# A half score tile moved ahead of a whole one, and its ordering moved from GpSimd to TensorE

## The chip, the cores and the metric

The kernel runs on one core of a Trainium2 chip. A core has five engines that run side by side and signal each other through semaphores: TensorE (PE in the profile, with its weight loads listed apart as PEld), VectorE (DVE), ScalarE (ACT), GpSimd (POOL) and SyncE (SP, which here issues DMAs). The metric is device time in microseconds (us), the median of several runs. The profile is one execution recorded by the hardware profiler.

## The reference

One transformer block on 2048 tokens of width 512, in float32: a layer norm, an attention block A of 32 heads of width 16, a gated path B, and their product added to the input.

```python
def _A_ref(x, wqkv, wo):
    qkv = (x @ wqkv).reshape(B, S, 3, H, Dh).transpose(2, 0, 3, 1, 4)
    q, k, v = qkv[0], qkv[1], qkv[2]
    scores = jnp.einsum("bhqd,bhkd->bhqk", q, k) * (Dh ** -0.5)
    p = _softmax(scores, axis=-1)
    o = jnp.einsum("bhqk,bhkd->bhqd", p, v)
    return o.transpose(0, 2, 1, 3).reshape(B, S, D) @ wo

def _B_ref(x, w1, b1, w2, b2):
    h = _gelu(jnp.einsum("bsd,df->bsf", x, w1) + b1)
    return jnp.einsum("bsf,fd->bsd", h, w2) + b2

xn = _layernorm(A_x)
s = _A_ref(xn, A_wqkv, A_wo)
g = _silu(_B_ref(xn, B_w1, B_b1, B_w2, B_b2))
return A_x + s * g
```

## The kernel before

The whole program is written out instruction by instruction in Python, under a manual schedule: each engine executes its instructions in the order of the text. Three parts follow each other. Up to about 478 us the norm, the projections and path B are made. From there to about 1506 us runs the attention loop in the form that the change touches. A last part finishes the attention and multiplies by `wo`.

Attention is done by units: 32 units, each of four heads (a group) and 512 queries. A softmax needs the largest score of each row before the exponentials are taken, so the scores are made twice. The first time ("S" work) they are made with the queries on the partitions, into a tile of 128 x 512 called `ps` in PSUM, and VectorE takes row maxima from it (`s_max`, line 189; it reduces two halves of 256 columns at a time). The second time ("T" work) they are made transposed, with keys on the partitions and the maximum already subtracted through two extra rows of the operands; ScalarE takes the exponential out of PSUM (`t_one`, matmul at line 740, exponential at line 742). Then the exponentials are multiplied by the values ("V" work, `pv_step`, line 805). The S work is done about nine units ahead of the T work.

Heads have width 16, so with the split of float32 into a high and a low part a score contracts over 48 rows (S) or 50 rows (T). One such matmul fills less than half of the array's 128 rows. The kernel therefore places head `a=0` at rows 0 to 63 and head `a=1` at rows 64 to 127, and orders the work so that matmuls on the two row halves stand next to each other.

The loop has a step for each 128 keys of a unit, 16 steps to a unit. A step is a string of letters, read from left to right:

- `T`: one transposed score tile and its exponential. The four of a step use the halves a = 1, 1, 0, 0.
- `S`: one whole score tile, 512 columns, and its reduce. The first `S` of a step takes the head a=0, the second the head a=1 of the same job.
- `X` and `Y`: a third score tile that two heads share. `X` writes the head a=0 into columns 0 to 255, `Y` the head a=1 into columns 256 to 511 of the same PSUM bank; then one reduce reads both. Two steps finish such a job.
- `V`: four matmuls of 32 columns each, that use the array's four column groups.

Since X and Y write one bank from two row halves, Y must not run beside X. Before the change this is ensured by a marker on GpSimd: an empty instruction (line 221) that waits until X is done, and Y waits for the marker. `run_off` then emits small GpSimd work that was put off (copies of the row maxima, lines 251 and 252).

PSUM banks: S, X and Y use three banks in a ring (`s_ring`: `ps_a`, `ps_b`, `ps_x`); X takes one out of the ring, and Y puts it back at the end. The T tiles use four banks in turn, and V has one. A score tile that is made into a bank waits for the reduce that read it last; a T tile waits for the exponential.

At the end of each unit ScalarE copies the result of V out of its bank (line 812). Some steps also hold a transpose of the row maxima (line 268) and a last reduction over them (line 248). GpSimd issues key loads (lines 109 and 112) and divisions (line 843) at fixed places of the order.

```python
ORDER = {0: "TTTTV", 3: "TXSTTSTYV"}
for op in ORDER[want] if n > 1 else ("TTTTV", "TTSTSVT")[n]:
    if op in "SXY":
        s_op(op)
```

Of the kernel before, what the change touches and what calls it, by code (L numbers as in the profile page):

```python
# [36 lines left out]
FILL0 = 30  # L37
HB = 4
W2B = 2
ORDER = {0: "TTTTV", 3: "TXSTTSTYV"}  # L40
HC = CH // 2
PAIRED = 28
KB = 3
# [5 lines left out]
def fused(ctx: ExitStack, tc: tile.TileContext, x, wqk, wv, wo, w1, b1, w2, b2, out):  # L49
    nc = tc.nc  # L50
# [35 lines left out]
    SYNC = mybir.DependencyInfo(mybir.DependencyClass.Sync, mybir.DependencyReason.DATA)  # L86
# [5 lines left out]
    def s_tile(held=False):  # L92
        pool = s_ring.pop(0)
        if not held:
            s_ring.append(pool)
        return pool.tile([P, CH], F32, name="ps"), pool
# [58 lines left out]
    done = {u: 0 for u in range(NU)}  # L155
# [16 lines left out]
    def at_of(job):  # L172
        u, st, p = job
        return divmod(st, NCH) if u % (NCH * KB) else divmod(st, NCH)[::-1]

    def s_mm(ps, job, a, c0, k0, w):
        u, st, p = job
        qi, ki = at_of(job)
        if u not in MX:
            MX[u] = qring.tile([P, GH, NCH, NCH, 2], F32, name="mx")  # L180
        r = slice(64 * a, 64 * a + 3 * DH)
        k0 += ki * CH
        return nc.tensor.matmul(ps[:, c0:c0 + w], QS[u][r, p, qi * P:(qi + 1) * P],  # L183
                                kts[u // NCH % KB][p][r, k0:k0 + w], start=True, stop=True).ins

    def s_max(ps, job, heads, parts):
        u, p = job[0], job[2]
        qi, ki = at_of(job)
        nc.vector.tensor_reduce(MX[u][:, 2 * p:2 * p + 2, qi, ki][:, heads, parts], ps.rearrange("p (n c) -> p n c", c=HC), axis=AX.X, op=OP.max)  # L189
        done[u] += 1  # L190
        if ended:
            s_end0(ended.pop())
        if done[u] == 64:
            ended.append(u)
        if done[NU - 1] == 64:
            s_end0(ended.pop())

    def s_whole(job, a):
        ps = s_tile()[0]
        s_mm(ps, job, a, 0, 0, CH)  # L200
        s_max(ps, job, a, slice(0, 2))
# [5 lines left out]
    jobs, whole, cut, put_off = [], [], [], []  # L207

    def s_op(op):
        if op == "S":  # L210
            if whole:
                s_whole(whole.pop(), 1)
            else:
                whole.append(jobs.pop(0))
                s_whole(whole[0], 0)
        elif op == "X":
            if not cut:
                cut[:] = [jobs.pop(0), 0]
            ps, pool = s_tile(True)
            x = s_mm(ps, cut[0], 0, 0, cut[1] * HC, HC)  # L220
            token = nc.gpsimd.nop().ins
            tc.add_manual_dep(token, x.name, SYNC, reason="row tile done")
            cut[2:] = [ps, pool, token]
            run_off()
        else:
            job, n, ps, pool, token = cut
            y = s_mm(ps, job, 1, HC, n * HC, HC)
            tc.add_manual_dep(y, token.name, SYNC, reason="other row tile")
            s_max(ps, job, slice(0, 2), n)
            s_ring.append(pool)  # L230
            cut[1] += 1
            if n:
                cut.clear()

    def run_off():
        while put_off:
            put_off.pop(0)()
# [76 lines left out]
    for j in range(len(pairs)):  # L314
        for h in range(2):
# [9 lines left out]
            n = 2 if nd < len(parts) and parts[nd][2] and ready - nd > room else 1  # L325
            n = max(n, need - 2 * (left - 1))
# [233 lines left out]
    s_when, put, row = [], [0], [0, 0]  # L560
# [387 lines left out]
    for t in range(NW):  # L948
        n = DONE + 2 * t
# [6 lines left out]
    for i, t in enumerate(late):  # L956
        n = L - 2 * len(late) - 1 + 2 * i
# [9 lines left out]
    for n in range(L + 1):  # L967
        ua, ka = divmod(n, 16)
        want = due(n) - due(n - 1)
        i = 0  # L970
# [3 lines that stand above are left out]
            elif op == "V":  # L974
                if n:
                    pv_step(*divmod(n - 1, 16))
                for _ in range(4):
                    tick()
                flush()
            else:  # L980
                if EARLY <= 4 * n + i < 4 * L:
                    t_one(ua, ka, i % 2, 1 - i // 2)
                for f, args in todo.get((n, i), []):
                    f(*args)
                i += 1
# [54 lines left out]
```

## Time and profile before

| | us |
|---|---|
| median of 3 runs | 1596.2 |
| lowest and highest run | 1596.11, 1596.48 |
| span of the profiled execution | 1594.7 |
| TensorE busy | 1587.6 |
| VectorE busy | 1382.8 |
| ScalarE busy | 1260.1 |
| GpSimd busy | 373.0 |

The profiled execution's own time is its span; the runs' times also hold what lies around it. The page gives busy time, then tenths of busy time in 40 slices, the chain of work that ended last, and groups of instructions. In the rows of a group or of the timeline, `ps<-kt,slot` is the output and the inputs by the program's names. A row of the timeline starts with start time and length in us, then engine, line, operation, names, shapes and count; in square brackets stands how long the engine was idle before it and what ended that. Matmul ends are modelled by the profiler, not observed. In the view of one line, the columns are the count, then the shortest, median and longest duration in ns, then the start of the first and of the last. In the view by stretches, the columns are the stretch, its length, the busy time and count of TensorE's matmuls, its weight loads, VectorE, ScalarE and GpSimd, the granted TensorE clock, the DMA share and GB/s.

### The profile page before, as it was taken

Reading aid. Unit: us, or ns where it says so; the run is one execution under the profiler, and the core shown is the slowest. Engines: PE = TensorE matmul, PEld = TensorE weight load, DVE = VectorE, ACT = ScalarE, POOL = GpSimd, SP = SyncE. Lnnn points to the kernel's source line nnn. Section 1 sums busy time; section 2 is a strip of 40 time slices with the busy share of each in tenths; the row PEclk is TensorE's granted clock in tenths of the full one; section 3 lists DMA queues with packets and bytes.
Section 4 is the critical chain, followed back from the end, with each engine's and each line's share of the span. In section 5 each row is a group of like instructions: output and inputs, shape, how many; then the busy total and the mean of one; then the engine's idle time right before and its main releaser. Section 6 shows DMA issues by size and latency. Waiting matters only on the chain.

```text
span 1594.7 us, 32234 instructions
## 1 busy us (share of the span) xinstructions
PE 1587.6 (100%) x12144; PEld 913.2 (57%) x12144; DVE 1382.8 (87%) x2261; ACT 1260.1 (79%) x2520; POOL 373.0 (23%) x394
## 2 busy tenths in 40 slices
PE   9999999999999999999999999999999999999998
PEld 8899999999884444444444444444444444444445
DVE  7598898989888999999999989999999999999735
ACT  4324333434349999999999999999999999999984
POOL 4145575756650001000100200100010000000142
PEclk9999999999999999999999999999999999999999
DMA  6626343454431113111410411311131111110252
GB/s 205 150 59 164 106 135 107 158 140 123 126 93 54 32 35 66 29 39 44 82 30 21 71 40 30 61 39 29 31 70 30 31 29 36 36 29 22 59 192 100
DMA packets 74651, 116.89 MB, mean 73 GB/s; under 512 B 23012, under 2 KB 24292, under 8 KB 73320
## 3 DMA queue, kind: packets, MB, share of 16 engines
q1 hardware_dynamic: 70748, 101.89, 22.8%
q0 software_dynamic: 3264, 12.35, 3.9%
q8 instruction: 96, 1.57, 0.4%
q14 instruction: 59, 0.48, 0.1%
q10 hardware_dynamic: 484, 0.60, 0.1%
HBM read 84.35 MB, written 25.97 MB: 69 GB/s over the span
## 4 chain that ended last, share of the span: by engine, by line
PE 98%; DVE 1%; DMA 1%; POOL 0%; issue 0%; ACT 0%; SPq 0%; DVEq 0%; POOLq 0%
PE pv L805 32%; PE ps L183 18%; PE pst L740 16%; PE ps L591 12%; PE pst L591 7%; PE ps L740 5%; PE ps L80 3%; PE pv L591 2%; PE ps L459 1%; PE pst L80 1%; DMA raw<-in_wqk 0%; DVE st L418 0%; PE pst L441 0%; DMA xt<-in_x 0%; PE pst L459 0%
## 5 line engine op out<-in xcount | busy, mean ns | idle before, releaser
L189 DVE TENSOR_REDUCE mx<-ps 128x2 f32<-128x512 f32 x2048 | 1299.5, 685 | 149.4 <-PE ps L183 68.8
L742 ACT ACTIVATE slot<-pst 128x512 f32<-128x512 f32 x1533 | 831.0, 612 | 21.6 <-PE pst L740 12.7
L805 PE MATMUL pv<-slot,vsb 128*32 128x512 f32 x4096 | 545.3, 605 | 0.0
L183 PE MATMUL ps<-kt,slot 48*128 48x512 f32 (+1 forms) x1364 | 393.5, 376 | 0.0
L740 PE MATMUL pst<-qt,kt 50*128 50x512 f32 x1149 | 372.7, 432 | 0.6 <-DVE gt L673 0.4
L740 PEld LDWEIGHTS pst<-qt,kt 50*128 50x128 f32 x1149 | 178.6, 184 | 279.9 <-ACT slot L742 264.3
L742 ACT ACTIVATE slot<-ps 128x512 f32<-128x512 f32 x515 | 315.5, 613 | 3.7 <-PE ps L740 0.5
L183 PEld LDWEIGHTS ps<-kt,slot 48*128 48x128 f32 x1364 | 210.6, 184 | 34.8 <-DVE mx L189 21.6
L591 PE MATMUL ps<-slot,w1h 64*128 64x512 f32 x1088 | 218.0, 393 | 0.2 <-ACT junk L605 0.2
L183 PE MATMUL ps<-kt,qz 48*128 48x512 f32 x512 | 212.4, 415 | 0.0
L183 PE MATMUL ps<-slot,slot 48*128 48x512 f32 (+1 forms) x598 | 172.8, 376 | 0.0
L740 PE MATMUL ps<-qt,kt 50*128 50x512 f32 x387 | 160.3, 416 | 0.0
L591 PEld LDWEIGHTS ps<-slot,w1h 64*128 64x128 f32 x1088 | 151.4, 185 | 8.3 <-ACT junk L605 2.7
L805 PEld LDWEIGHTS pv<-slot,vsb 128*32 128x32 f32 x4096 | 80.6, 108 | 120.2 <-issue 112.2
L591 PE MATMUL ps<-slot,w1l 64*128 64x512 f32 x544 | 141.7, 393 | 0.0
L378 POOL TENSOR_TENSOR hl<-hg,hh 128x512 fp32r<-128x512 f32 x76 | 96.7, 1295 | 129.6 <-ACT hh L377 82.5
L605 ACT ACTIVATE junk<-ident_r 1x1 f32<-1x1 f32 x92 | 18.0, 196 | 120.8 <-PE pst L591 113.6
L740 PE MATMUL pst<-qt,slot 50*128 50x512 f32 x384 | 112.5, 415 | 0.0
L251 POOL CAST nmh<-nm 128x16 fp32r<-128x16 f32 x32 | 6.3, 197 | 413.7 <-PE pst L740 184.7
L183 PEld LDWEIGHTS ps<-kt,qz 48*128 48x128 f32 x512 | 93.7, 183 | 16.3
L183 PEld LDWEIGHTS ps<-slot,slot 48*128 48x128 f32 x598 | 92.5, 184 | 15.7 <-DVE mx L189 10.9
L740 PEld LDWEIGHTS ps<-qt,kt 50*128 50x128 f32 x387 | 71.1, 184 | 44.0 <-ACT slot L742 42.8
(159 smaller groups left out, 1699.7 us busy)
## 6 DMA issues: line engine op xcount, KB each, us to landing
raw<-in_w SPq DMA_DIRECT2D x88, 256.0 KB
qk_h<-hh SPq DMA_DIRECT2D x32, 256.0 KB
qk_l<-hl SPq DMA_DIRECT2D x32, 256.0 KB
qt<-qk_h SPq DMA_DIRECT2D x128, 64.0 KB
slot<-qk_h SPq DMA_DIRECT2D x92, 64.0 KB
g_d<-gt POOLq DMA_DIRECT2D x16, 256.0 KB, 3.5
qt<-qk_l SPq DMA_DIRECT2D x64, 64.0 KB
dn<-den_d SPq DMA_DIRECT2D x32, 128.0 KB
```

Source lines behind the costliest of these rows:

```text
L80: nc.tensor.matmul(ps, lhs[a], rhs[b], start=first and n == 0, stop=last and n == 2)
L183: return nc.tensor.matmul(ps[:, c0:c0 + w], QS[u][r, p, qi * P:(qi + 1) * P], kts[u // NCH % KB][p][r, k0:k0 + w], start=True, stop=True).ins
L189: nc.vector.tensor_reduce(MX[u][:, 2 * p:2 * p + 2, qi, ki][:, heads, parts], ps.rearrange("p (n c) -> p n c", c=HC), axis=AX.X, op=OP.max)
L251: nc.gpsimd.tensor_copy(hl[:, 0], nm)
L378: nc.gpsimd.tensor_sub(hl, raw, hh.bitcast(F32))
L459: nc.tensor.matmul(pq["q", g, c], W1[g][i][:, k * P:(k + 1) * P], (xh, xl)[j][c][:, k], start=n == 0 and k == 0, stop=n == 2 and k == KT - 1)
L591: i = nc.tensor.matmul(ps, lhs[r], rhs[r], start=first, stop=last).ins
L605: i = nc.scalar.activation(junk[:, :1], ident_r[:1, :1].bitcast(F32), AF.Copy).ins
L740: nc.tensor.matmul(ps, kts[g % KB][p][r, k * P:(k + 1) * P], QT[u][r, p, :], start=True, stop=True)
L742: nc.scalar.activation(PT[u, k][:, 2 * p + a, :], ps, AF.Exp, scale=SCALE)
L805: nc.tensor.matmul(PV[u][32 * j:32 * j + 32, :], vsb[:, k, h:h + 32], PT[u, k][:, j, :], start=(k == 0), stop=(k == NT - 1))
```

## The change

The step's order becomes `TXSTTYSTV`: Y stands directly behind the third T tile and ahead of the second S. The GpSimd marker is removed. In its place an empty TensorE instruction, called `hold`, is put directly ahead of Y; it waits until X is done, on the semaphore that TensorE's own matmuls raise. The maxima of the shared tile are now emitted ahead of those of the second S, and X's bank goes back into the ring ahead of the second S.

```diff
-ORDER = {0: "TTTTV", 3: "TXSTTSTYV"}
+ORDER = {0: "TTTTV", 3: "TXSTTYSTV"}
...
             x = s_mm(ps, cut[0], 0, 0, cut[1] * HC, HC)
-            token = nc.gpsimd.nop().ins
-            tc.add_manual_dep(token, x.name, SYNC, reason="row tile done")
-            cut[2:] = [ps, pool, token]
+            cut[2:] = [ps, pool, x]
             run_off()
         else:
-            job, n, ps, pool, token = cut
-            y = s_mm(ps, job, 1, HC, n * HC, HC)
-            tc.add_manual_dep(y, token.name, SYNC, reason="other row tile")
+            job, n, ps, pool, x = cut
+            hold = nc.tensor.nop().ins
+            tc.add_manual_dep(hold, x.name, SYNC, reason="row tile done")
+            s_mm(ps, job, 1, HC, n * HC, HC)
             s_max(ps, job, slice(0, 2), n)
             s_ring.append(pool)
             cut[1] += 1
```

## The prediction

> **What bounds the kernel now.** First the page: its head, engine shares, granted clock and the chain that ended last.
>
> ```profile
> span 1594.7 us, 32234 instructions
> ...
> PE 1587.6 (100%) x12144; PEld 913.2 (57%) x12144; DVE 1382.8 (87%) x2261; ACT 1260.1 (79%) x2520; POOL 373.0 (23%) x394
> ...
> PEclk9999999999999999999999999999999999999999
> ...
> PE 98%; DVE 1%; DMA 1%; POOL 0%; issue 0%; ACT 0%; SPq 0%; DVEq 0%; POOLq 0%
> ```
>
> TensorE is the chain, at full clock. A busy PE is not a PE at its peak, so the question is where it stands still inside a step. Next, the line of the POOL marker, which runs once in each step that the change touches, and the stretch of these steps.
>
> ```profile
> L221 POOLq EVENT_SEMAPHORE  x490: 17/17/17, 479.6 to 1505.8; - x164
> ...
> 478.00:1506.30 1028.30, 1028.19 (x7860) 439.98 (x7862) 936.60 (x1538) 1012.25 (x1992) 76.74 (x128) 1.00 0.18 41
> ```
>
> 490 markers from 479.6 to 1505.8 make 489 steps of 1026.2 / 489 = 2.099 us: 64% of the span. ACT (the fourth busy column) and DVE (the third) are nearly full in it too, so they have to be watched. Now the weight loads of one such step, in order of time.
>
> ```profile
> 902.76 0.18 PEld L740 LDWEIGHTS pst<-qt,kt 50*128 50x128 f32 x1 [0.84 <-ACT slot L742]
> 902.76 0.18 PEld L183 LDWEIGHTS ps<-kt,slot 48*128 48x128 f32 x1
> 902.87 0.19 PEld L740 LDWEIGHTS pst<-qt,kt 50*128 50x128 f32 x1
> 902.87 0.19 PEld L183 LDWEIGHTS ps<-kt,slot 48*128 48x128 f32 x1
> 902.99 0.18 PEld L740 LDWEIGHTS pst<-qt,kt 50*128 50x128 f32 x1
> 903.30 0.18 PEld L183 LDWEIGHTS ps<-kt,slot 48*128 48x128 f32 x1
> 903.35 0.18 PEld L740 LDWEIGHTS ps<-qt,kt 50*128 50x128 f32 x1
> 903.41 0.19 PEld L183 LDWEIGHTS ps<-kt,slot 48*128 48x128 f32 x1
> 903.85 0.16 PEld L805 LDWEIGHTS pv<-slot,vsb 128*32 128x32 f32 x8 [0.25 <-issue]
> 904.85 0.18 PEld L740 LDWEIGHTS pst<-qt,kt 50*128 50x128 f32 x1 [0.84 <-ACT slot L742]
> ```
>
> I call the pieces T0, X, S0, T1, T2, S1, T3, Y, V, in program order (S0 and S1 are the two heads' whole tiles). Lower row half of the array: X, S0, T2, T3; upper: T0, T1, S1, Y; the halves work side by side (T0 and X load at the same 902.76). Loads run T0 and X 902.76, T1 and S0 902.87, T2 902.99, then a hole, S1 903.30, T3 903.35, Y 903.41, and V from 903.85 to 904.85: a constant 1.00. Who ends the hole:
>
> ```profile
> 902.57 0.68 DVE L189 TENSOR_REDUCE mx<-ps 128x2 f32<-128x512 f32 x1
> 902.68 0.62 ACT L742 ACTIVATE slot<-ps 128x512 f32<-128x512 f32 x1
> 902.76 0.50 PE L740 MATMUL pst<-qt,kt 50*128 50x512 f32 x1
> 902.76 0.18 PEld L183 LDWEIGHTS ps<-kt,slot 48*128 48x128 f32 x1
> 902.77 0.38 PE L183 MATMUL ps<-kt,slot 48*128 48x256 f32 x1
> ...
> 903.42 1.89 DVE L189 TENSOR_REDUCE mx<-ps 128x2 f32<-128x512 f32 x3 [0.17 <-PE ps L183]
> ```
>
> The third reduce of the step before ends at 902.57 + 0.68 = 903.25 and frees S1's bank: S1's load starts 0.05 later. The same 0.05 stands between the end of T3's older exponential (903.30) and T3's load. The three reduces take 1.89 from S0's arrival, so a short step is followed by a late S1. This shows in neighbouring steps, by V's first load:
>
> ```profile
> 901.76 0.16 PEld L805 LDWEIGHTS pv<-slot,vsb 128*32 128x32 f32 x8 [0.25 <-issue]
> ...
> 905.90 0.16 PEld L805 LDWEIGHTS pv<-slot,vsb 128*32 128x32 f32 x8 [0.23 <-issue]
> ```
>
> 905.90 - 901.76 = 4.14 for two steps, 2.07 each. A step in which S1 doesn't wait:
>
> ```profile
> 817.01 0.18 PEld L740 LDWEIGHTS ps<-qt,slot 50*128 50x128 f32 x1 [0.84 <-ACT slot L742]
> ...
> 817.35 0.18 PEld L183 LDWEIGHTS ps<-kt,slot 48*128 48x128 f32 x1
> ...
> 819.03 0.18 PEld L740 LDWEIGHTS ps<-qt,slot 50*128 50x128 f32 x1 [0.84 <-ACT slot L742]
> ```
>
> 819.03 - 817.01 = 2.02 is TensorE's floor. The last kind is the long step after a unit's end, when ACT has the copy of line 812 to do as well and T3 waits for ACT:
>
> ```profile
> 545.32 0.16 PEld L805 LDWEIGHTS pv<-slot,vsb 128*32 128x32 f32 x8 [0.25 <-ACT os L812]
> ...
> 547.28 0.18 PEld L740 LDWEIGHTS ps<-qt,kt 50*128 50x128 f32 x1 [0.30 <-ACT slot L742]
> ...
> 547.71 0.16 PEld L805 LDWEIGHTS pv<-slot,vsb 128*32 128x32 f32 x8 [0.24 <-issue]
> ...
> L812 ACT ACTIVATE os<-pv 128x512 f32<-128x512 f32 x30 | 18.8, 628 | 0.0
> ```
>
> Its length is 2.39, and 30 of them are 71.7 us. The other 459 steps hold 1026.2 - 71.7 = 954.5, a mean of 2.079. Last, T3's load is followed by V 0.43 later: the price of a whole tile whose weights come last.
>
> **The change part by part.** *Y ahead of S1.* In the upper half the order becomes T0, T1, Y, S1. Y's bank is X's own, so Y waits for no reduce. S1's load moves later by what Y takes, so DVE's release of S1's bank (0.54 after T0's load above) is covered. This part alone would bring steps towards the floor. DVE and ACT do the same work; banks still come free in the order of the reduces (S0, halves, S1 instead of S0, S1, halves), so each of the next tiles waits for the reduce of the same place in the order.
>
> *The marker goes.* 490 POOL instructions of 17 ns vanish. Queued behind them on POOL are the maxima's copies, the divisions and key loads, which may go earlier; none is on the chain (POOL 0% above). I take nothing for it.
>
> *The hold.* TensorE now waits until X has signalled, and Y, S1, T3, V and all after them are queued behind it. So the price is X's signal. When does that come? Two rows, the first asked for the stretch 903.32 to 903.34 alone:
>
> ```profile
> L221 POOLq EVENT_SEMAPHORE  x1: 17/17/17, 903.3 to 903.3; - x1
> ...
> 903.30 0.60 ACT L742 ACTIVATE slot<-pst 128x512 f32<-128x512 f32 x1
> ...
> 903.10 0.51 PE L740 MATMUL pst<-qt,kt 50*128 50x512 f32 x2
> ```
>
> X's own modelled end is 902.77 + 0.38 = 903.15, but the marker, which waits for nothing but X, runs at 903.33, just behind ACT's exponential on T0 (903.30; T0's modelled end is 903.26). So X, half as long, signals behind T0, which was issued ahead of it. The Trainium skill, "TensorE: Matmul & The Clock Gate", Part 3, The mechanism, says that matmuls start and end in strict program order. By that rule X cannot signal ahead of T0 and the sum is the slow one below; by X's modelled end, Y's load could start at 903.20 and the sum would be the floor's, 1572 us.
>
> Now the new step, counted from T0's load. Y's load follows the signal as S1 and T3 follow theirs: about 903.35, 0.59. S1's load follows Y's by 0.11, as S0's (902.87) follows X's (902.76): 0.70. There the price of a late whole tile applies, 0.43 to V: 1.13. With V's 1.00 the step is **2.13** whatever DVE does. T3 starts beside S1 in the other half and ends with it; ACT's release of T3's bank (0.59 above) is covered.
>
> Sum. 459 steps x 2.13 = 977.7. To it come the passes of line 268, which push T0, and with it X's signal, later:
>
> ```profile
> 528.57 0.16 PEld L805 LDWEIGHTS pv<-slot,vsb 128*32 128x32 f32 x8 [0.25 <-issue]
> ...
> 529.76 0.18 PEld L740 LDWEIGHTS pst<-qt,kt 50*128 50x128 f32 x1
> ...
> L268 PE MATMUL pst<-ident_r,nmh 128*64 128x128 f32 (+1 forms) x9 | 2.4, 268 | 0.0
> ...
> L268 PE MATMUL ps<-ident_r,nmh 128*64 128x128 f32 (+1 forms) x4 | 1.1, 267 | 0.0
> ```
>
> T0's load stands 1.19 behind V's instead of 1.00, 13 times: 2.6. The long steps hang on ACT, which gains up to 2.13 - 2.02 = 0.11 in the short step ahead, so I take 2.39 - 0.11 = 2.28: 68.4. Total 977.7 + 2.6 + 68.4 = 1048.7 against 1026.2: +22.5 us. The profiled span is 1594.7; the runs' median, 1596.2, lies 1.5 above it, what lies around the span. 1596.2 + 22.5 = **1619 us**.
>
> *The hold's own cost.* No row shows such a wait of TensorE on itself. Lower bound: it rides on Y's weight load as the marker's wait does now, cost nothing; that is the sum above, and I take it, since Y's load then has no other wait to carry. Upper bound: it is an instruction of its own, as at line 441 (asked for 18.36 to 18.38; then the load behind it):
>
> ```profile
> L441 PEldq EVENT_SEMAPHORE  x1: 51/51/51, 18.4 to 18.4; - x1
> ...
> 18.45 0.14 PEld L441 LDWEIGHTS ps<-ident,xn 128*128 128x128 f32 x1 [0.72 <-PE ps L459]
> ```
>
> The load comes 0.08 behind the wait's start. With a start like the marker's, Y loads at 903.41, 0.65, and the step is 2.19.
>
> **The rivals.** *A wait as an own instruction (A2).* 459 x 2.19 + 2.6 + 30 x 2.22 = 1074.4: +48, **1644 us**. For it: line 441's wait does stand alone. Against it: by the kernel's text, Y's load has no other wait left to carry, and the marker's wait, which it carries now, is gone.
>
> *Faster: the hold is free (B).* If X's signal reaches TensorE so that Y loads by 0.48 (1.00 + 0.48 + 0.11 + 0.43 = 2.02), the order alone counts: 459 x 2.02 + 2.6 + 71.7 = 1001.5, -24.7, **1572 us**. Break-even is a load at 0.54 (903.30). For it: X's modelled end, and that a wait on one's own queue could be met early or be dropped as already in order, so that the change does not do what it says. Against it: the marker's time, later than that point.
>
> *The hold empties TensorE (C).* If it waits for all that was issued, T2 (modelled end 903.61 above) lets Y load at 903.66, 0.90; every step is 2.44 and the sum is 489 x 2.44 + 2.6 = 1195.8: **1766 us**. The skill's "PSUM — Partial Sum Buffer", Engine vs sequencer instructions, says that a nop is the sequencer's and waits for earlier instructions to be dispatched only. By that rule this doesn't happen; no run here shows it.
>
> **How the numbers follow.** Forecast 0.62 (1612 to 1628 for itself: 0.02 either way in Y's load is 9 us), A2 0.18, B 0.11, between B and the forecast, within 0.2% of before (3 us, about what a measurement here can tell), 0.03, C and all that is slower than A2 0.06. The range from 1612 to 1650 takes in the forecast and A2, 0.80. Faster 0.11, same 0.03, slower 0.86 (0.62 + 0.18 + 0.06).
>
> **What would show it.** In the profile after: no line 221 on POOL; S1's load no longer behind a reduce; a hole between T2's and Y's loads ending about 0.59 behind T0's load (0.65: A2; 0.48 or less: B; 0.90: C); plain steps all alike near 2.13 instead of 2.02 and 2.12 in turn; long steps shorter than 2.39. Wrong it would be above all if X's signal came earlier than the POOL marker suggests.

## The result, and the profile after

The changed kernel takes 1619.16 us (median of 4 runs, 1618.95 to 1619.55) against 1596.15 us: a ratio of 1.0145, 95% interval 1.0133 to 1.0158. It is 23.0 us slower; the profiled span, 1617.7 us, is also 23.0 us longer than before.

The page of the kernel after, the lines that answer to those shown of before:

```profile
span 1617.7 us, 31752 instructions
...
PE 1611.4 (100%) x12144; PEld 908.4 (56%) x12144; DVE 1381.0 (85%) x2261; ACT 1268.5 (78%) x2520; POOL 373.1 (23%) x394
...
PEclk9999999999999999999999999999999999999999
...
PE 99%; DVE 1%; DMA 0%; issue 0%; ACT 0%; DVEq 0%
...
L183 PEld LDWEIGHTS ps<-kt,slot 48*128 48x128 f32 x1364 | 201.2, 185 | 55.6 <-PE pst L739 35.9
```

The work is the same (12144 matmuls, 2261 VectorE and 2520 ScalarE instructions) and so is the clock. TensorE is still the chain. What has changed is the last line, by its idle time and what ended it. The same group on the page of the kernel before:

```profile
L183 PEld LDWEIGHTS ps<-kt,slot 48*128 48x128 f32 x1364 | 210.6, 184 | 34.8 <-DVE mx L189 21.6
```

This is the larger of two groups of line 183. It idled 34.8 us with DVE the main releaser; now it idles 55.6 us, and the main releaser is TensorE itself. The attribution to line 739 (the T tiles) is inferred by the profile; the wait put into the program is on X. Lines behind the edit are one lower than before: 739 is T, 741 its exponential, 804 V, 811 the copy at a unit's end.

TensorE's weight loads in two steps of the kernel after, in order of time (start, length, operation, what ended the idle time ahead):

```profile
901.75 0.18 PEld L739 LDWEIGHTS pst<-qt,kt 50*128 50x128 f32 x1 [0.84 <-ACT slot L741]
901.76 0.18 PEld L183 LDWEIGHTS ps<-kt,slot 48*128 48x128 f32 x1
901.86 0.19 PEld L739 LDWEIGHTS pst<-qt,kt 50*128 50x128 f32 x1
901.87 0.19 PEld L183 LDWEIGHTS ps<-kt,slot 48*128 48x128 f32 x1
901.98 0.18 PEld L739 LDWEIGHTS pst<-qt,kt 50*128 50x128 f32 x1
902.34 0.18 PEld L183 LDWEIGHTS ps<-kt,slot 48*128 48x128 f32 x1 [0.18 <-PE pst L739]
902.35 0.18 PEld L739 LDWEIGHTS ps<-qt,kt 50*128 50x128 f32 x1
902.45 0.19 PEld L183 LDWEIGHTS ps<-kt,slot 48*128 48x128 f32 x1
902.89 0.16 PEld L804 LDWEIGHTS pv<-slot,vsb 128*32 128x32 f32 x8 [0.25 <-issue]
903.89 0.18 PEld L739 LDWEIGHTS pst<-qt,kt 50*128 50x128 f32 x1 [0.84 <-ACT slot L741]
...
905.02 0.16 PEld L804 LDWEIGHTS pv<-slot,vsb 128*32 128x32 f32 x8 [0.25 <-issue]
...
907.16 0.16 PEld L804 LDWEIGHTS pv<-slot,vsb 128*32 128x32 f32 x8 [0.25 <-issue]
```

The loads now come as T0, X, T1, S0, T2, then a hole, Y at 902.34, T3, S1 at 902.45, V. (In the program S0 still stands ahead of T1.) Y loads 0.59 behind T0, S1 0.11 behind Y, V 0.44 behind S1. From V to V it is 905.02 - 902.89 = 2.13 and 907.16 - 905.02 = 2.14: the alternation of 2.02 and 2.12 is gone, and the plain steps are as long as the longer of the two were: measured from V to V, 440 of the 490 steps of the loop take 2.12 to 2.15. The reduce that used to hold S1 back, in the timeline of VectorE after:

```profile
901.48 0.68 DVE L189 TENSOR_REDUCE mx<-ps 128x2 f32<-128x512 f32 x1
```

It ends at 902.16, 0.29 ahead of S1's load. So the wait that the new order was able to cover is covered, and another one, longer, has come into the step ahead of it. The long step after a unit's end, after:

```profile
546.94 0.16 PEld L804 LDWEIGHTS pv<-slot,vsb 128*32 128x32 f32 x8 [0.25 <-ACT os L811]
...
548.78 0.18 PEld L739 LDWEIGHTS ps<-qt,kt 50*128 50x128 f32 x1
549.20 0.16 PEld L804 LDWEIGHTS pv<-slot,vsb 128*32 128x32 f32 x8 [0.24 <-issue]
```

It takes 549.20 - 546.94 = 2.26 us, where it took 2.39; the mean of all 30 is 2.255.

### The profile page after: what moved, and what is told of

Same layout as the page of the kernel before. It is cut to its first block, busy times and chain, and to the rows that moved or that the text cites. A ratio compares the mean times of both kernels' runs of the same rounds, so it can differ in the third digit from the quotient of the medians.

```text
span 1617.7 us, 31752 instructions
## 1 busy us (share of the span) xinstructions
PE 1611.4 (100%) x12144; PEld 908.4 (56%) x12144; DVE 1381.0 (85%) x2261; ACT 1268.5 (78%) x2520; POOL 373.1 (23%) x394
## 4 chain that ended last, share of the span: by engine, by line
PE 99%; DVE 1%; DMA 0%; issue 0%; ACT 0%; DVEq 0%
PE pv L804 32%; PE ps L183 19%; PE pst L739 16%; PE ps L590 12%; PE pst L590 7%; PE ps L739 5%; PE ps L80 3%; PE pv L590 2%; PE ps L458 1%; PE pst L80 1%; DVE st L417 0%; DMA xt<-in_x 0%; PE pst L440 0%; PE pst L458 0%; DVE slot L75 0%; DVE xn L431 0%
## 5 line engine op out<-in xcount | busy, mean ns | idle before, releaser
L183 PE MATMUL ps<-kt,slot 48*128 48x256 f32 (+1 forms) x1364 | 410.0, 387 | 0.0
L739 PE MATMUL pst<-qt,kt 50*128 50x512 f32 x1149 | 368.0, 428 | 0.5 <-DVE gt L672 0.4
L183 PEld LDWEIGHTS ps<-kt,slot 48*128 48x128 f32 x1364 | 201.2, 185 | 55.6 <-PE pst L739 35.9
L183 PE MATMUL ps<-slot,slot 48*128 48x256 f32 (+1 forms) x598 | 179.9, 387 | 0.0
L183 PEld LDWEIGHTS ps<-slot,slot 48*128 48x128 f32 x598 | 88.5, 184 | 24.9 <-PE pst L739 19.9
```

The costliest lines, as they stand in the source:

```text
L739: nc.tensor.matmul(ps, kts[g % KB][p][r, k * P:(k + 1) * P], QT[u][r, p, :], start=True, stop=True)
```

## The experiments

The theory to test: the price is the time at which X's signal comes, and that is late because X was issued behind the longer T0; the hold passes it on at hardly any cost, and every step ends a fixed time behind Y's load. Two rivals: a wait of TensorE on its own semaphore costs a fixed stall, wherever X stands; or the new order is bad by itself, through its banks and reduces. The expectations call these the signal theory, the self-wait theory and the order theory. Each experiment has a kernel of before on the same chip beside it, at 1596.15 to 1596.34 us.

### X first

```diff
 (against the changed kernel)
-ORDER = {0: "TTTTV", 3: "TXSTTYSTV"}
+ORDER = {0: "TTTTV", 3: "XTSTTYSTV"}
```

> The changed kernel with X issued one place earlier, ahead of the first T tile (order XTSTTYSTV). Signal theory (the stall of Y is X's signal, which comes behind that of the longer T tile issued ahead of it): X is now the first of the pair and signals at its own end, about 0.41 us after the step's first weight load instead of 0.55; Y's weights load at about 0.45, below the 0.48 at which they stop mattering, and the steps fall from 2.13 to between 2.02 (TensorE's floor, total about 1572 us) and 2.04 (ACT's release of the last T bank becomes the next to be late: its load comes 1.63 after V at a 2.02 step, and 0.43 later is V; total about 1580 us). Self-wait theory (any wait of TensorE on its own semaphore costs a fixed stall of the queue): no change, steps of 2.13, about 1619 us. Order theory (Y ahead of the second S is what costs, by its banks and reduces): about 1619 us too.

Measured: 1583.46 us, ratio to before 0.9920 (0.9905 to 0.9935). It is 35.7 us faster than the changed kernel by swapping two neighbours, and faster than the kernel before. Its weight loads, with the row of ScalarE that matters:

```profile
685.23 0.16 PEld L804 LDWEIGHTS pv<-slot,vsb 128*32 128x32 f32 x8 [0.26 <-issue]
686.22 0.18 PEld L183 LDWEIGHTS ps<-kt,slot 48*128 48x128 f32 x1 [0.84 <-DVE mx L189]
...
686.66 0.33 PEld L183 LDWEIGHTS ps<-kt,slot 48*128 48x128 f32 x2
686.86 0.18 PEld L739 LDWEIGHTS pst<-qt,kt 50*128 50x128 f32 x1
687.29 0.16 PEld L804 LDWEIGHTS pv<-slot,vsb 128*32 128x32 f32 x8 [0.25 <-issue]
...
689.31 0.16 PEld L804 LDWEIGHTS pv<-slot,vsb 128*32 128x32 f32 x8 [0.25 <-issue]
```

```profile
686.19 0.62 ACT L741 ACTIVATE slot<-pst 128x512 f32<-128x512 f32 x1
```

Y loads (first of the two at 686.66) 0.44 behind the step's first load instead of 0.59. Both rivals said 1619; they fall here. What is late next also shows: the older exponential ends at 686.81, T3's load follows at 686.86 and V 0.43 later. That step takes 687.29 - 685.23 = 2.06; the next, to 689.31, is at the floor again, 2.02. The total lies 3.5 us above the upper end that was expected, 1580. Most of that is in the plain steps: from V to V, 447 of them take 2.046 us in the mean, not 2.04, which is 2.7 us. The long steps take 2.39, as they did before the change.

### The order alone, with the GpSimd marker

```diff
 (against the kernel before)
-ORDER = {0: "TTTTV", 3: "TXSTTSTYV"}
+ORDER = {0: "TTTTV", 3: "TXSTTYSTV"}
```

> The new order alone, with the GpSimd marker of before in place of the TensorE wait. Signal theory: the marker adds a second signal (in the trace of before it runs 0.57 after the step's first load and Y's weights follow 0.06 to 0.08 later), so Y loads at about 0.64 instead of 0.59, the step is 1.00 + 0.64 + 0.11 + 0.43 = 2.18 and the total about 1640 us: slower than the whole change. Self-wait theory: the stall is the self-wait's, so without it the order's gain shows: about 1575 us. Order theory: as slow as the change, about 1619 us.

Measured: 1639.73 us, ratio 1.0272 (1.0252 to 1.0293), on the signal theory's number.

```profile
903.57 0.18 PEld L740 LDWEIGHTS pst<-qt,kt 50*128 50x128 f32 x1 [0.84 <-ACT slot L742]
...
904.20 0.18 PEld L183 LDWEIGHTS ps<-kt,slot 48*128 48x128 f32 x1 [0.22 <-POOLq L221]
...
904.74 0.16 PEld L805 LDWEIGHTS pv<-slot,vsb 128*32 128x32 f32 x8 [0.25 <-issue]
```

Here the profile names the marker of line 221 as what ends the hole, at 0.63. So the new order costs 43.4 us with the marker (1639.73 - 1596.34), and in that order putting the wait on TensorE gives back 20.6 of it (1639.73 - 1619.16).

### The hold alone, in the old order

```diff
 (against the changed kernel)
-ORDER = {0: "TTTTV", 3: "TXSTTYSTV"}
+ORDER = {0: "TTTTV", 3: "TXSTTSTYV"}
```

> The TensorE wait alone, in the old order (Y last ahead of V). Signal theory: Y is issued behind S1 and T3, whose loads come at 0.54 to 0.59 and later after the step's first load, so X's signal has long come; steps alternate between 2.02 and 2.12 as before: 1594 to 1597 us. Self-wait theory: the fixed stall stands ahead of Y and V, each step 0.05 or more longer: about 1619 us or more. Order theory: 1596 us.

Measured: 1596.40 us, ratio 1.0000 (0.9991 to 1.0010). The page names the reduce as S1's releaser, as before the change:

```profile
L183 PEld LDWEIGHTS ps<-kt,slot 48*128 48x128 f32 x1364 | 205.4, 184 | 34.5 <-DVE mx L189 23.5
```

The wait is in the program here too, on Y's matmul. A wait of TensorE on itself that is already met when it is reached costs nothing that can be measured here; the self-wait theory falls a second time.

### The wait on a later tile

```diff
 (against the changed kernel)
+        last[:] = [s_mm(ps, job, a, 0, 0, CH)]
-        s_mm(ps, job, a, 0, 0, CH)
...
-            tc.add_manual_dep(hold, x.name, SYNC, reason="row tile done")
+            tc.add_manual_dep(hold, last[0].name, SYNC, reason="row tile done")
```

> The changed kernel with the wait put on the whole tile S0, issued behind X, instead of on X; order and count of instructions are the same. Signal theory: S0's signal comes about 0.09 after X's (a whole tile behind a half one in the lower row half), Y's weights load at about 0.67 to 0.68, and every plain step grows by the same 0.09 to about 2.21: about 1657 us. Self-wait theory: the stall is that of the wait as such, no change: about 1619 us. Order theory: about 1619 us.

Measured: 1657.83 us, ratio 1.0385 (1.0365 to 1.0406).

```profile
903.13 0.18 PEld L739 LDWEIGHTS ps<-qt,kt 50*128 50x128 f32 x1 [0.84 <-ACT slot L741]
...
903.80 0.18 PEld L183 LDWEIGHTS ps<-kt,slot 48*128 48x128 f32 x1 [0.26 <-PE ps L183]
...
904.35 0.16 PEld L804 LDWEIGHTS pv<-slot,vsb 128*32 128x32 f32 x8 [0.25 <-issue]
```

Same instructions, same order; only the signal that is waited for stands later, and Y loads at 0.67. The step follows the signal.

### The wait as an instruction of its own

```diff
 (against the changed kernel)
-            hold = nc.tensor.nop().ins
+            hold = nc.tensor.nop(nofuse=True).ins
```

> The changed kernel with the wait kept as an instruction of its own (the empty instruction is told not to be merged into the weight load behind it). Signal theory with the price of line 441: the load comes 0.08 behind the start of such a wait instead of 0.05 behind the signal, Y loads at about 0.65 instead of 0.59, the step is about 2.19 and the total about 1644 us (the prediction's rival A2). If a wait standing alone costs no more than one on the load: 1619 us. If such an instruction holds the queue for longer than its row shows: above 1660 us.

Measured: 1645.70 us, ratio 1.0310 (1.0289 to 1.0331). The line of the wait and the loads of a step:

```profile
L225 PEldq EVENT_SEMAPHORE  x490: 51/51/51, 479.2 to 1554.9; - x164
...
905.53 0.18 PEld L739 LDWEIGHTS pst<-qt,kt 50*128 50x128 f32 x1 [0.84 <-ACT slot L741]
...
906.18 0.18 PEld L183 LDWEIGHTS ps<-kt,slot 48*128 48x128 f32 x1 [0.23 <-issue]
```

490 waits of 51 ns appear that the changed kernel's profile does not have, and Y loads at 0.65. That is the prediction's rival A2, at 1645.7 where it was priced at 1644. In the change itself, then, the wait rides on Y's weight load.

### X first, with the marker

```diff
 (against the kernel before)
-ORDER = {0: "TTTTV", 3: "TXSTTSTYV"}
+ORDER = {0: "TTTTV", 3: "XTSTTYSTV"}
```

> X ahead of the first T tile and Y ahead of the second S, but with the GpSimd marker of before in place of the TensorE wait. Signal theory: X signals at about 0.40, the marker passes it on 0.09 later, Y loads at 0.49, the step by Y is 1.00 + 0.49 + 0.11 + 0.43 = 2.03, below the mean of 2.04 that ACT's release sets; so the marker costs next to nothing here: 1583 to 1588 us. Rival (the TensorE wait is itself part of the gain, the marker costs in any order what it cost in the changed order, about 20 us): about 1604 us.

Measured: 1583.98 us, ratio 0.9923 (0.9906 to 0.9939).

```profile
686.61 0.18 PEld L183 LDWEIGHTS ps<-kt,slot 48*128 48x128 f32 x1 [0.84 <-DVE mx L189]
...
687.10 0.29 PEld L183 LDWEIGHTS ps<-kt,slot 48*128 48x128 f32 x2
687.24 0.18 PEld L740 LDWEIGHTS pst<-qt,kt 50*128 50x128 f32 x1
687.66 0.16 PEld L805 LDWEIGHTS pv<-slot,vsb 128*32 128x32 f32 x8 [0.24 <-issue]
```

Y loads at 0.49, T3 at 0.63, and V comes 0.42 behind T3. The same detour that cost 20.6 us is hidden here, since the release of T3's bank by ACT is later than it.

### X first alone

```diff
 (against the kernel before)
-ORDER = {0: "TTTTV", 3: "TXSTTSTYV"}
+ORDER = {0: "TTTTV", 3: "XTSTTSTYV"}
```

> X ahead of the first T tile alone: marker and Y's place at the end as before. Signal theory: Y was not waiting for X in this order, and S1 still waits for the third reduce of the step before, so steps alternate between 2.02 and 2.12 as before: 1595 to 1597 us. Rival (X's early place is a gain by itself, through the first loads of the step or the banks): about 1584 us.

Measured: 1595.39 us, ratio 0.9995 (0.9986 to 1.0005): no difference. V's first loads in neighbouring steps still alternate, 2.13 and 2.01:

```profile
687.42 0.16 PEld L805 LDWEIGHTS pv<-slot,vsb 128*32 128x32 f32 x8 [0.25 <-issue]
689.55 0.16 PEld L805 LDWEIGHTS pv<-slot,vsb 128*32 128x32 f32 x8 [0.25 <-issue]
691.56 0.16 PEld L805 LDWEIGHTS pv<-slot,vsb 128*32 128x32 f32 x8 [0.25 <-issue]
```

This run also times X's signal without any wait of TensorE. The marker waits for nothing but X. Its line in the stretch 688.84 to 688.85 alone, in the step whose first load is at 688.42:

```profile
L221 POOLq EVENT_SEMAPHORE  x1: 17/17/17, 688.8 to 688.8; - x1
```

It runs 0.42 behind the step's first load, where before the change it ran at 0.57 (903.33 - 902.76). So the swap alone brings X's signal 0.15 forward, and here nothing in the step uses it. The gain of X first comes only together with Y ahead of S1: the early signal makes it possible for Y to go there, and Y there covers the reduce.

### What is late next

```diff
 (against "X first")
+            if "seen" not in prog:
+                nc.gpsimd.memset(PT[u, k][:, :, 448:], 1.0)
...
-        nc.scalar.activation(PT[u, k][:, 2 * p + a, :], ps, AF.Exp, scale=SCALE)
+        w = CH if "seen" in prog else 448
+        nc.scalar.activation(PT[u, k][:, 2 * p + a, :w], ps[:, :w], AF.Exp, scale=SCALE)
```

> X first with the TensorE wait, and in the loop each exponential takes 448 of its 512 columns; GpSimd writes ones into the other 64, so one eighth of the exponentials is left out. This asks what is late next when X is first. If it is ACT's release of the last T bank (T3's weights follow the end of the older exponential by 0.05): the exponential's pitch falls by the time of 64 columns, about 0.05, four of them give 0.2 a step, T3's bank is free early, plain steps all stand near TensorE's floor of 2.02 instead of 2.02 and 2.06 in turn, the long steps fall by about 0.2 as well, total about 1565 us. If it is something else (the third reduce or Y's wait): steps stay at 2.04 in the mean and only the long steps shorten, about 1577 us.

Measured: 1563.98 us, ratio 0.9798 (0.9769 to 0.9826).

```profile
687.42 0.16 PEld L807 LDWEIGHTS pv<-slot,vsb 128*32 128x32 f32 x8 [0.25 <-issue]
...
688.86 0.33 PEld L183 LDWEIGHTS ps<-kt,slot 48*128 48x128 f32 x2
689.01 0.18 PEld L741 LDWEIGHTS pst<-qt,kt 50*128 50x128 f32 x1
689.44 0.16 PEld L807 LDWEIGHTS pv<-slot,vsb 128*32 128x32 f32 x8 [0.26 <-issue]
...
691.45 0.16 PEld L807 LDWEIGHTS pv<-slot,vsb 128*32 128x32 f32 x8 [0.24 <-issue]
```

With a shorter exponential T3 loads 0.15 behind Y (0.20 in the longer step of "X first" above), and two steps in a row take 2.02 and 2.01 where "X first" alternates between 2.06 and 2.02. The exponentials were what kept "X first" from the floor. How much they fill the loop is shown by the stretch from 500 to 1450 us, in the kernels "the change", "X first", "X first, with the marker" and this one:

```profile
500.00:1450.00 950.00, 950.00 (x7104) 392.56 (x7100) 846.13 (x1390) 922.91 (x1801) 71.57 (x119) 1.00 0.20 40
...
500.00:1450.00 950.00, 950.00 (x7355) 427.05 (x7351) 875.76 (x1438) 945.14 (x1865) 72.88 (x120) 1.00 0.20 41
...
500.00:1450.00 950.00, 950.00 (x7348) 408.18 (x7348) 875.35 (x1437) 945.29 (x1863) 73.36 (x120) 1.00 0.18 41
...
500.00:1450.00 950.00, 950.00 (x7500) 426.30 (x7496) 892.21 (x1469) 877.05 (x1900) 217.06 (x591) 1.00 0.18 41
```

With X first ScalarE (the fourth busy column) works 945.1 of 950.0 us, with the marker 945.3: it sets the pace, and a step that ends early only makes the next one wait. This run also adds GpSimd work (the last busy column), on which ScalarE waits for some 60 us in this stretch, so it shows that the exponentials' length was the limit, not what exactly 64 columns are worth.

### All runs with Y ahead of S1, by Y's load

| kernel | Y's load behind the step's first, us | time, us |
|---|---|---|
| X first | 0.44 | 1583.46 |
| X first, marker | 0.49 | 1583.98 |
| the change | 0.59 | 1619.16 |
| order alone, marker | 0.63 | 1639.73 |
| own instruction | 0.65 | 1645.70 |
| wait on S0 | 0.67 | 1657.83 |

At 0.44 and 0.49 the total is nearly the same, since there ScalarE sets the pace. From 0.59 on each step grows with Y's load: from 0.59 to 0.67 the total grows by 38.7 us, or 0.079 for each of 489 steps.

## Why the prediction was right

**The bound and the steps.** TensorE's chain and the two-step alternation were read rightly: the hold alone and X first alone leave both as they were, at 1596.40 and 1595.39 us.

**The hold's price.** This step carried the forecast: X's signal comes behind T0's, against X's own modelled end. It gave Y's load at 0.59, S1's at 0.70, V's at 1.13 and steps of 2.13. The profile after has 0.59, 0.70, 1.14 and 2.13 to 2.14. That the order of issue, and not X's length or the wait, makes the signal late is shown by X first: with the same X and the same wait, X one place earlier, Y loads 0.15 earlier. The marker shows the same by itself, 0.42 against 0.57. What the runs don't tell apart is whether X's work was over at its modelled end and its signal came later, or whether its work itself ended later; the ends of matmuls are modelled.

One of the two signs from which the prediction read this doesn't bear on it. ACT's exponential on T0 starts at 903.30 because the exponential ahead of it ends there (902.68 + 0.62), so its start doesn't say when T0's signal came. The marker at 903.33 carries the step alone.

**The sum.** +22.5 us were forecast and +23.0 measured. It is not a sum of errors that cancel: from V to V the 447 plain steps take 2.132 us in the mean (2.13 forecast), the 30 long ones 2.255 (2.28), and the 13 with a pass of line 268 stand 0.19 above a plain one, at 2.326. Two small slips don't matter: 13 passes of 0.19 are 2.5 us, not 2.6, and 9 us either way of 1619 would begin at 1610, not at 1612. The hold as an instruction of its own was priced at +48 and costs 49.6 (1645.70 - 1596.15).

**Where it was off.** The rival on the other side, B, was priced at 1572 us as if TensorE's floor were reached as soon as Y loads by 0.48. X first fulfils that condition (0.44) and takes 1583.46. The rival's weak step is "the order alone counts": for the forecast it was asked what would be late next, for the rival it wasn't. ACT's release of T3's bank, which the prediction had beside S1's in the trace of before (T3's load at 0.59, S1's at 0.54 behind T0's), takes over, since ScalarE is then busy nearly all the time; the run with shorter exponentials shows it. The prediction took nothing for the marker's going. In the old order that is what was measured (1596.40 against 1596.34); in the new one the marker in place of the hold costs 20.6 us more.

**Rival C**, a hold that empties TensorE, would load Y at 0.90. It loads at 0.59, and at 0.67 when the wait is put on S0, so the hold waits for the tile that it names and not for all that was issued.

## What to carry to other kernels

The modelled end of a matmul is not the time from which it can be waited for: before a wait is put on a short matmul, look at what was issued ahead of it on the other row tile, and try issuing first the one that is waited for. A piece that is moved forward to cover a wait brings its own wait along, so lay that wait's release time beside the place that it moves to; here the whole difference between 23 us lost and 13 us won (1596.34 - 1583.46) is one swap of two neighbours. When a stall is removed, name for each rival too what is late next: here ScalarE, busy 945.1 of 950.0 us, was reached before TensorE's floor.

## What the runs showed of the hardware that was not expected

X, 256 columns, and T0, 512 columns, run on different row halves and start together, yet X's modelled end in the trace (0.39 behind the step's first load before the change) is not when it can be waited for: Y's load, which needs it, went at 0.59 behind T0 and at 0.44 when X was issued first. The Trainium skill, "TensorE: Matmul & The Clock Gate", Part 3, The mechanism, has matmuls end in program order, and both runs agree with it. The modelled ends of the profile do not show this for these two tiles on different row halves: before the change X's is 903.15, ahead of T0's 903.26.

A wait of TensorE on its own semaphore was not dropped as already in order, and where it rides on a weight load and is already met it cost nothing that shows (1596.40 against 1596.34). Standing alone, at 51 ns in the profile, it moved Y's load from 0.59 to 0.65.
